# RWKV-7 recurrence with a SoLU MLP on one core: weight fetches moved to another queue and earlier, and four issue orders changed

## The chip, the cores and the metric

The kernel runs on one core of a Trainium2 chip. A core has five engines that each work through their own instruction list in order: TensorE (PE in the profile, with its weight loads as PEld), VectorE (DVE), ScalarE (ACT), GpSimd (POOL) and SyncE (SP), which here only starts transfers. SyncE and ScalarE each have a queue from which they issue DMA transfers (SPq and ACTq in the profile). An engine that meets an instruction whose inputs aren't ready waits, and everything behind that instruction on the same engine waits too. The metric is the device time of one execution in microseconds (us), as the median of several runs.

## The reference

The first block is a linear recurrence over 768 time steps, for 4 batches of 8 heads with head dimension 40. The second is an MLP over the 3072 tokens that come out (320 features each), with 1024 hidden units.

```python
for t in range(S):                       # r, k, v, w, a, b: (4, 8, 768, 40)
    y[:, :, t] = np.einsum('bhd,bhde->bhe', rt, state)
    Sa = np.einsum('bhde,bhe->bhd', state, at)
    state = state * wt[:, :, None, :] - np.einsum('bhd,bhe->bhde', Sa, bt) \
            + np.einsum('bhd,bhe->bhde', vt, kt)
x = y.transpose(0, 2, 1, 3).reshape(3072, 320)
h = x @ w_in                             # 320 x 1024
e = np.exp(h - max(h)); solu = h * e / (sum(e) + 1e-9)
ln = (solu - mean(solu)) / sqrt(var(solu) + 1e-6) * g_ln
out = ln @ w_out                         # 1024 x 320
```

The recurrence's inputs are float32. The two weight matrices arrive as 64-bit floats, and the kernel takes them apart into float32 itself.

## The kernel before

**The recurrence in chunks.** The 768 steps are cut into 12 rounds of 64 steps. A round is done as two *iterations*, each for two of the four batches, so the main loop has N = 24 iterations, i = 0 to 23. Within a chunk the recurrence becomes matrix products and the inverse of triangular 32x32 blocks. For one iteration there are these generator functions, each of which issues a bit of work per step and then yields:

- `front` (letters f and g in the order strings): decay factors, scaled keys, and the triangular blocks `nt`. It runs 5 iterations ahead.
- `scatter` and `gather`: the blocks go through memory so that 64 of them lie one per partition, and come back as `nb`.
- `invert` (I): for a whole round, 30 rows of two VectorE instructions each (L410, L412) on the tile `u`. The result goes to memory in two layouts, and `bring_inverse` fetches it as `tinvT` and `tinv`. Lines 400 to 404 prepare `u`: VectorE fills its first half, GpSimd zeroes its second half (L402) and sets that half's diagonal to one.
- `attend` (a): transposes `kT`, `vT`, `rT` (ScalarE copies them out of PSUM at L259) and the products `psi`, `lamv`, `px0`.
- `solve` (s): completes the 64x64 inverse from 32x32 blocks (`py`, `pz`).
- `recurrence` (r): the serial chain from iteration to iteration. Its first step adds the carried part on VectorE (L525, the tile `x0`, shown as `x`), its third step multiplies by the inverse (`pu`, L544), and later steps update the state `sm`.
- `readout` (y): the outputs of the chunk, multiplied on VectorE (L597, tile `x`) and repacked by DMA for the MLP.

**The MLP.** It runs 6 iterations behind (LAG = 6). `hidden` (h, and b once the iteration is over) has nine steps: five that issue the six products of `h` (L618), the fifth of which also takes the row maximum on VectorE (L628); then the exponential on ScalarE (L632); then q = h times exp on VectorE (L635), written over `e`; then two for the statistics (L640 to L650). The PSUM tile `h` is there only once, so the next MLP's products wait for q. `output` (o) transposes q (L658, copied by ScalarE at L659), multiplies by `w_out` (L663), and scales on ScalarE into `osb` (L668).

**The weights.** `weights` (W) fetches 26 pieces, each into one of four landing tiles, and turns each into float32 by two VectorE instructions (L162, L164), three ScalarE ones (L167 to L169), one more on VectorE (L171) and two on GpSimd (L174, L175). A piece's fetch is issued two pieces ahead, on SyncE's queue (L211). One piece takes two steps of W. After the last, `w_out` is scaled by g and its weighted column mean is taken off: a copy of g (L235), 16 products (`mean`, L238) and eight VectorE instructions (L240).

**The order.** Nothing is scheduled by the compiler: under `manual_schedule` the program order on each engine is what the order strings say. `turns` goes through a string and runs one step of the named generator for each letter (for I the number that `inverse_steps` gives). Iterations 0 to 5 use an EARLY string, later ones STEADY. After the loop six MLPs are left, with a string of their own. Before the loop a prologue computes the first two rounds' fronts, the first inverse and iteration 0's `attend` and `solve`. It is written out in the body of the `with` block:

```python
turns("a a I", dict(I=99), a=at, I=inv)
bring_inverse(0, nc.scalar)
turns("a a a f g f g a f g", {}, f=f, g=g, a=at)
...
ws, after, before = weights(), None, None
```

Here the first inverse is fetched on ScalarE's queue, and `weights` begins only in the loop.

Of the kernel before, what the change touches and what calls it, by code (L numbers as in the profile page):

```python
# [52 lines left out]
def kernel(  # L53
# [94 lines left out]
    def bank(name):  # L148
        return ps1.tile([P, 512], FP32, tag="bank", name=name)
# [28 lines left out]
    def weights():  # L178

        nc.sync.dma_start(out=g_rows, in_=moe_g_ln.rearrange("(c p) -> c p", p=P))
        pieces, hw, hm = [], DFF // 2, DM // 2
        for at in range(0, hw, 256):
            cols = slice(at, at + 256)
            for p in range(2):
                for j in range(2):
                    src = slice(j * hw + at, j * hw + at + 256)
                    pieces.append((w_in[:, 2 * p + j, cols], [moe_w_in[p * hm:p * hm + P, src]]))
            pieces.append((w_in[:, 4, cols], [moe_w_in[p * hm + P:p * hm + hm, j * hw + at:j * hw + at + 256]  # L190
                                              for j in range(2) for p in range(2)]))
        for c in range(NF):
            for at in range(0, DM, 160):
                cols = slice(at, at + 160)
                pieces.append((w2[:, c, cols], [moe_w_out[c * P:(c + 1) * P, cols]]))
        exact = moe_w_in.dtype == FP32
        land, temps = [], []
        if not exact:
            for tag in ("e", "lnT"):
                x = two.tile([P, 512], I64, tag=tag, name="bits", bufs=1)  # L200
                land += [x[:, 0:256], x[:, 256:512]]
            temps = [two.tile([P, 2, 256], I32, tag=tag, name="parts", bufs=1) for tag in ("osb", "parts")]

        def fetch(j):
            if j >= len(pieces):
                return
            dst, parts = pieces[j]
            to = dst if exact else land[j % 4][0:dst.shape[0], 0:dst.shape[1]]
            row = 0
            for part in parts:  # L210
                nc.sync.dma_start(out=to[row:row + part.shape[0]], in_=part)  # L211
                row += part.shape[0]

        for j in range(2):
            fetch(j)
        yield
        open_ = None
        for j, (dst, _) in enumerate(pieces):
            new = None if exact else narrow(dst, land[j % 4], temps[j % 2])
            for _ in range(2):  # L220
                for part in (open_, new):
                    if part:
                        next(part)
                if _:
                    fetch(j + 2)
                yield
            open_ = new
        for _ in range(2):
            if open_:
                next(open_)  # L230
        pg = bank("pg")
        nc.tensor.transpose(out=pg[:, 0:NF], in_=g_rows, identity=ident[0:NF, 0:NF])
        nc.scalar.copy(out=g_col, in_=pg[:, 0:NF])
        gb = two.tile([P, NF, P], FP32, tag="e", name="gb", bufs=1)
        nc.scalar.mul(out=gb, in_=g_col.unsqueeze(2).to_broadcast([P, NF, P]), mul=1.0 / DFF)  # L235
        mean = bank("mean")
        for c in range(NF):
            nc.tensor.matmul(mean[:, 0:DM], lhsT=gb[:, c, :], rhs=w2[:, c, :], start=c == 0, stop=c == NF - 1)  # L238
        for c in range(NF):
            nc.vector.scalar_tensor_tensor(out=w2[:, c, :], in0=w2[:, c, :], scalar=g_col[:, c:c + 1],  # L240
                                           in1=mean[:, 0:DM], op0=ALU.mult, op1=ALU.subtract)
            yield

    def half(p):
        return slice(64 * p, 64 * p + 64)
# [148 lines left out]
    def invert(n):  # L394

        nb = of_round[n]["nb"]
        u = two.tile([P, Q // 2, Q], FP32, tag="u", name="u", bufs=1)
        nc.vector.tensor_scalar(out=u[half(0)], in0=nb[half(0)].rearrange("b (c z) t -> b c z t", z=2)[:, :, 0],  # L400
                                scalar1=-1.0, scalar2=None, op0=ALU.mult)
        nc.gpsimd.memset(u[half(1)], 0.0)  # L402
        for p, engine in enumerate((nc.vector, nc.gpsimd)):
            engine.memset(u[half(p)].rearrange("b c t -> b (c t)")[:, p:Q * Q // 2:Q + 2], 1.0)  # L404
        yield
        for j in range(1, Q - 1):
            m, rows = Q - 1 - j, (j + 1) // 2
            t = two.tile([P, Q * Q // 8], FP32, tag="prod", name="prod", bufs=1)[:, 0:rows * m] \
                .rearrange("p (c r) -> p c r", c=rows)
            nc.vector.tensor_tensor(out=t, in0=nb[:, j:j + 1, j + 1:Q].to_broadcast([P, rows, m]),  # L410
                                    in1=u[:, 0:rows, j:j + 1].to_broadcast([P, rows, m]), op=ALU.mult)
            nc.vector.tensor_tensor(out=u[:, 0:rows, j + 1:Q], in0=u[:, 0:rows, j + 1:Q], in1=t, op=ALU.subtract)  # L412
            yield
        u_dram = of_round[n]["u"] = dram.tile([64, Q, Q], FP32, tag="u_dram", name="u_dram")
        for p in range(2):
            nc.sync.dma_start(out=u_dram.rearrange("b (c z) t -> b c z t", z=2)[:, :, p], in_=u[half(p)])
        ut = two.tile([P, Q, Q // 2], FP32, tag="ut", name="ut", bufs=1)
        nc.vector.tensor_copy(out=ut, in_=u.rearrange("p c t -> p t c"))
        ut_dram = of_round[n]["ut"] = dram.tile([P, Q, Q // 2], FP32, tag="ut_dram", name="ut_dram")
        nc.sync.dma_start(out=ut_dram, in_=ut)  # L420
        yield
# [267 lines left out]
    def fronts(i):  # L689

        return [j for j in ((4, 5) if i == 0 else (i + AHEAD,)) if j < N]

    EARLY = ("r r a r f r W I r W y W r I W W a f L a s W a f W a W I f I W s f W a f",
             "r r a r f g r W I r W y W r I W W a f g L a s W a f g W a W I f g I W s f g W a f g")
    STEADY = "r r b b a r f o r o I o r o y o r I o a f L h a s a h f a I h f I s h f h a f h h"
    front_of = {}

    front_of = {}
# [22 lines left out]
    with tc.manual_schedule():  # L721
        load(0, "w", "a", "b", "k")
        f, g = front(0), front(1)
        turns("f g", {}, f=f, g=g)
        load(1, "w", "a")
        turns("f g", {}, f=f, g=g)
        load(1, "b")
        turns("f f f f g g g g f g", {}, f=f, g=g)
        scatter(0)
        gather(0)  # L730
        load(0, "v", "r")
        load(1, "k")
        f, g, at, inv, so = front(2), front(3), attend(0), invert(0), solve(0)
        turns("f g f g f f g g", {}, f=f, g=g)
        load(2, "w", "a", "b", "k")
        turns("a a I", dict(I=99), a=at, I=inv)
        bring_inverse(0, nc.scalar)
        turns("a a a f g f g a f g", {}, f=f, g=g, a=at)
        scatter(1)
        gather(1)  # L740
        load(1, "v", "r")
        begin(0)
        turns("s s", {}, s=so)
        inv = inverses()
        ws, after, before = weights(), None, None
        for i in range(N):
            m, more, js = i - LAG, i + 1 < N, fronts(i)
            if i % 2 and (i + 3) // 2 < NCH:
                gather((i + 3) // 2)
            if i == 1:  # L750
                steps(inv, 8)
            now = hidden(m) if m >= 0 else None
            parts = dict(r=recurrence(i), y=readout(i), I=inv, W=ws, h=now, b=after, o=before)
            parts.update(zip("fg", (front_of[j] for j in js)))
            if more:
                bring_inverse(i + 1)
                parts.update(a=attend(i + 1), s=solve(i + 1))
            if i % 2 == 0:
                load((i + 6) // 2, "w", "a")
                parts["L"] = later((i + 6) // 2)  # L760
            turns(EARLY[len(js) - 1] if i < LAG else STEADY, dict(I=inverse_steps(i)), **parts)
            if i % 2:
                load((i + 3) // 2, "v", "r")
                repack(i // 2)
            if js and js[-1] % 2:
                scatter(js[-1] // 2)
            begin(i + 1)
            after, before = now, output(m) if m >= 0 else None
            if i == LAG - 1:
                steps(ws, 99)  # L770
        for m in range(N - LAG, N):
            now = hidden(m)
            turns("h h o o h h b b h o o o o h h", {}, h=now, b=after, o=before)
            after, before = now, output(m)
        turns("b b o o o o o o", {}, b=after, o=before)


# [28 lines left out]
```

## Time and profile before

The median is 848.69 us of 3 runs (846.84 to 854.91). The profiled execution spans 844.7 us. The trace was cut into stages at the first `pu` product of each iteration:

| stage | us | PE busy | DVE busy | granted PE clock |
|---|---|---|---|---|
| prologue, to the `pu` of iteration 0 | 0 to 66.7 | 25.2 | 26.8 | 0.74 |
| iteration 0 | 66.7 to 116.5 | 21.4 | 22.9 | 0.66 |
| iteration 1 | 116.5 to 151.3 | 18.7 | 20.0 | 0.75 |
| iterations 2 to 4 | 151.3 to 238.5 | 58.2 | 57.0 | 0.66 to 0.73 |
| iterations 5 and 6 | 238.5 to 297.9 | 43.3 | 34.0 | 0.82 and 0.99 |
| two steady iterations | 572.6 to 627.3 | 50.0 | 35.0 | 0.97 |
| iterations 19 to 22 | 627.3 to 723.4 | 85.0 | 46.7 | 0.97 |
| the last six MLPs | 738.7 to 844.7 | 78.5 | 29.9 | 0.85 |

Read it thus: where PE is busy for most of a stage (steady: 50.0 of 54.7 us), only PE's own gaps can be won. Where it isn't (everything up to iteration 5, and the end), the stage is as long as a chain through several engines and transfers, and the question is which wait ends last. The granted clock is the share of full speed that TensorE was given in the stage.

### The profile page before, as it was taken

To read this page: it belongs to the slowest core of one execution; us is meant where nothing else is said; L and a number is where in the kernel's file an instruction comes from. 1 tells how busy PE (TensorE), PEld (TensorE's weight loads), DVE (VectorE), ACT (ScalarE), POOL (GpSimd) and SP (SyncE) were. 2 spreads that over 40 slices of the span, in tenths; PEclk is the share of its full clock that TensorE was granted. 3 is DMA by queue.
4 is the path that set the end of the run, shared out by engine and by line. 5 is a ranking of instruction groups with operands and counts; after the bars stand their busy time and mean duration, and the time that the engine had idled before them with its cause. 6 is when DMAs were issued, how large, how long until landed. Compare 5 with 4: busy or idle time off the path is not lost.

```text
span 844.7 us, 28254 instructions
## 1 busy us (share of the span) xinstructions
PE 646.6 (77%) x12281; PEld 462.1 (55%) x12281; DVE 451.1 (53%) x1234; ACT 272.3 (32%) x631; POOL 126.3 (15%) x228
## 2 busy tenths in 40 slices
PE   6124364685666998989989989899898998868786
PEld 4123353564455666666666666566665666534343
DVE  3352484756744756666577575674766633332222
ACT  4012333343432333433443334433343323211211
POOL 4101323331330120111201110111001000000000
PEclk9658567776778998999999999999999999979878
DMA  9815535444561453534534435435134111000000
GB/s 133 134 35 101 117 64 109 93 94 102 104 116 26 78 100 53 109 70 84 104 64 87 88 61 102 84 72 101 21 79 73 43 34 25 15 21 1 16 16 16
DMA packets 269804, 60.02 MB, mean 71 GB/s; under 512 B 255464, under 2 KB 265328, under 8 KB 269680
## 3 DMA queue, kind: packets, MB, share of 16 engines
q1 hardware_dynamic: 268448, 57.91, 36.6%
q8 instruction: 97, 1.59, 0.8%
q10 hardware_dynamic: 1232, 0.30, 0.2%
q14 instruction: 27, 0.22, 0.1%
HBM read 40.08 MB, written 13.37 MB: 63 GB/s over the span
## 4 chain that ended last, share of the span: by engine, by line
PE 59%; DVE 14%; SPq 8%; DMA 6%; issue 6%; ACT 5%; POOL 0%; ACTq 0%; DVEq 0%; POOLq 0%
PE h L618 13%; PE po L663 13%; PE plnT L658 4%; DVE u L412 3%; DVE prod L410 3%; PE pcx L337 3%; DVE e L635 3%; PE pyo L590 2%; SPq L302 2%; PE py L478 2%; PE pst L570 2%; PE pu L544 2%; PE plamv L276 2%; PE pyo L504 2%; DVE nmax L628 2%
## 5 line engine op out<-in xcount | busy, mean ns | idle before, releaser
L618 PE MATMUL h<-w_in,xT 128*128 128x512 f32 (+1 forms) x288 | 135.5, 673 | 19.6 <-DVE e L635 16.5
L663 PE MATMUL po<-w,lnT 128*128 128x320 f32 x384 | 120.4, 446 | 0.0
L410 DVE TENSOR_TENSOR prod<-blk,u 128x30 f32<-128x30 f32 (+4 forms) x360 | 98.8, 274 | 29.5 <-POOL u L404 17.5
L412 DVE TENSOR_TENSOR u<-u,prod 128x30 f32<-128x30 f32 (+4 forms) x360 | 102.2, 284 | 12.4
L663 PEld LDWEIGHTS po<-w,lnT 128*128 128x128 f32 x384 | 69.2, 194 | 24.3 <-issue 3.5
L650 POOL TENSOR_TENSOR rs<-c,mhalf 128x1 f32<-128x1 f32 x24 | 13.2, 549 | 371.1 <-DVE c L649 348.4
L618 PEld LDWEIGHTS h<-w_in,xT 128*128 128x128 f32 (+1 forms) x288 | 40.1, 201 | 45.8 <-issue 42.3
L337 PE MATMUL pcx<-cst,lw 128*128 128x132 f32 x192 | 35.7, 320 | 27.1 <-ACT vT L259 22.8
L668 ACT ACTIVATE osb<-po,rs 128x320 f32<-128x320 f32 x24 | 12.6, 527 | 134.2 <-PE po L663 122.1
L628 DVE TENSOR_REDUCE nmax<-h 128x1 f32<-128x1024 f32 x24 | 29.3, 1223 | 48.9 <-PE h L618 48.9
L635 DVE TENSOR_TENSOR e<-h,e 128x1024 f32<-128x1024 f32 x24 | 29.4, 1225 | 44.1 <-ACT e L632 44.1
L337 PEld LDWEIGHTS pcx<-cst,lw 128*128 128x128 f32 x192 | 29.9, 215 | 39.3 <-ACT vT L259 23.2
L544 PE MATMUL pu<-tinvT,x 64*64 64x64 f32 x768 | 21.0, 250 | 36.4 <-DVE x L525 25.5
L659 ACT COPY lnT<-plnT 128x512 f32<-128x512 f32 x48 | 27.8, 587 | 63.2 <-PE plnT L658 62.9
L278 DVE TENSOR_TENSOR lamv<-plamv,cst 128x512 f32<-128x512 f32 x24 | 16.6, 692 | 56.5 <-PE plamv L276 56.5
L278 DVE TENSOR_TENSOR lamu<-plamu,cst 128x512 f32<-128x512 f32 x24 | 16.6, 691 | 48.2 <-PE plamu L276 48.2
L478 PE MATMUL py<-tinv,nt 32*32 32x32 f32 x768 | 19.8, 204 | 29.2 <-ACT vT L259 19.2
L544 PEld LDWEIGHTS pu<-tinvT,x 64*64 64x64 f32 x768 | 17.4, 155 | 42.5 <-DVE x L525 29.7
L658 PE MATMUL plnT<-cst,e 128*128 128x128 f32 x192 | 38.1, 342 | 3.2 <-DVE e L635 3.2
L597 DVE TENSOR_TENSOR x<-pyo,kx 128x512 f32<-128x512 f32 x24 | 16.6, 690 | 43.2 <-PE pyo L590 42.9
L276 PE MATMUL plamv<-rT,vT 64*64 64x64 f32 x768 | 19.1, 246 | 26.7 <-ACT rT L259 26.4
L658 PEld LDWEIGHTS plnT<-cst,e 128*128 128x128 f32 x192 | 29.0, 177 | 14.7 <-issue 10.7
(108 smaller groups left out, 1163.5 us busy)
## 6 DMA issues: line engine op xcount, KB each, us to landing
blk<-blk_dram SPq DMA_DIRECT2D x24, 256.0 KB
raw_w<-in_w_dram SPq DMA_DIRECT2D x24, 160.0 KB
raw_a<-in_a_dram SPq DMA_DIRECT2D x24, 160.0 KB
raw_b<-in_b_dram SPq DMA_DIRECT2D x24, 160.0 KB
raw_k<-in_k_dram SPq DMA_DIRECT2D x24, 160.0 KB
v<-in_v_dram SPq DMA_DIRECT2D x24, 160.0 KB
r<-in_r_dram SPq DMA_DIRECT2D x24, 160.0 KB
out_dram<-osb SPq DMA_DIRECT2D x24, 160.0 KB
```

The lines of the kernel that those rows point to most:

```text
L276: nc.tensor.matmul(t[half(c ^ p * cross), p, g * L:(g + 1) * L], lhsT=lhs[half(p), g, half(c)], rhs=rhs[half(p), g, half(c)], start=True, ...
L278: nc.vector.tensor_tensor(out=dst, in0=t[:, :, 0:G * L].rearrange("q p (g c) -> q p g c", g=G), in1=tri.unsqueeze(1).unsqueeze(1).to_broad ...
L337: nc.tensor.matmul(t[:, g * 132:g * 132 + 132], lhsT=pair(lw, 2 * j + g), rhs=cst[:, lo:lo + 132], start=True, stop=True)
L410: nc.vector.tensor_tensor(out=t, in0=nb[:, j:j + 1, j + 1:Q].to_broadcast([P, rows, m]), in1=u[:, 0:rows, j:j + 1].to_broadcast([P, rows, ...
L412: nc.vector.tensor_tensor(out=u[:, 0:rows, j + 1:Q], in0=u[:, 0:rows, j + 1:Q], in1=t, op=ALU.subtract)
L478: nc.tensor.matmul(t[quarter(out), c:c + Q], lhsT=lhs(p, g), rhs=rhs(p, g), start=True, stop=True)
L544: nc.tensor.matmul(t[half(z), c ^ p, h // 2 * L:h // 2 * L + L], lhsT=x0[half(c ^ p), h, :], rhs=d["tinvT"][half(c ^ p), p, h % G, :], sta ...
L618: nc.tensor.matmul(h[:, j * 512:j * 512 + 512], lhsT=of_round[i // 2]["xT"][rows, kt, i % 2 * P:i % 2 * P + P], rhs=w_in[rows, 4 if kt == ...
L628: nc.vector.tensor_reduce(out=nmax, in_=h, axis=AX.X, op=ALU.max, negate=True)
L635: nc.vector.tensor_tensor(out=q, in0=h, in1=e, op=ALU.mult)
L658: nc.tensor.transpose(out=t[:, j * P:(j + 1) * P], in_=q[:, f * P:(f + 1) * P], identity=ident)
L663: nc.tensor.matmul(o[:, 0:DM], lhsT=lnT[:, f, :], rhs=w2[:, f, :], start=f == 0, stop=f == NF - 1)
```

## The change

It has five parts, all of them of order or of the engine used; the arithmetic stays as it was.

1. The weights' transfers (32 fetches and g) are issued by ScalarE instead of SyncE. The first W step, which fetches g and the first two pieces, moves from iteration 0 into the prologue, so that the first piece has landed when it is needed. The EARLY strings have nine W each instead of ten.
2. In the prologue, `psi` and `rT` are issued before the first inverse is fetched on ScalarE's queue instead of after it; the other steps of `attend` alternate with the fronts.
3. In `invert`, the second half of `u` is cleared, and given its diagonal, on VectorE instead of GpSimd (for all twelve inverses).
4. In STEADY, q (the seventh step of `hidden`) moves behind the recurrence's first step of the next iteration, so that VectorE does the `x0` addition before q. The first step of `hidden` moves ahead. The steps `b` follow later. The centring of `w_out` gets two more yields (ahead of the mean's products and after them) and then takes two pieces per step; what is left of it when iteration 6 begins is issued there.
5. In the last six MLPs, the exponential is issued ahead of the four last `output` steps, and with that ahead of `osb`, instead of after them; q follows at the start of the next one.

```diff
-        nc.sync.dma_start(out=g_rows, in_=moe_g_ln.rearrange("(c p) -> c p", p=P))
+        nc.scalar.dma_start(out=g_rows, in_=moe_g_ln.rearrange("(c p) -> c p", p=P))
...
-                nc.sync.dma_start(out=to[row:row + part.shape[0]], in_=part)
+                nc.scalar.dma_start(out=to[row:row + part.shape[0]], in_=part)
...
         nc.scalar.mul(out=gb, in_=g_col.unsqueeze(2).to_broadcast([P, NF, P]), mul=1.0 / DFF)
+        yield
         mean = bank("mean")
         for c in range(NF):
             nc.tensor.matmul(mean[:, 0:DM], lhsT=gb[:, c, :], rhs=w2[:, c, :], start=c == 0, stop=c == NF - 1)
+        yield
         for c in range(NF):
             nc.vector.scalar_tensor_tensor(out=w2[:, c, :], in0=w2[:, c, :], scalar=g_col[:, c:c + 1],
                                            in1=mean[:, 0:DM], op0=ALU.mult, op1=ALU.subtract)
-            yield
+            if c % 2:
+                yield
...
-        nc.gpsimd.memset(u[half(1)], 0.0)
-        for p, engine in enumerate((nc.vector, nc.gpsimd)):
-            engine.memset(u[half(p)].rearrange("b c t -> b (c t)")[:, p:Q * Q // 2:Q + 2], 1.0)
+        nc.vector.memset(u[half(1)], 0.0)
+        for p in range(2):
+            nc.vector.memset(u[half(p)].rearrange("b c t -> b (c t)")[:, p:Q * Q // 2:Q + 2], 1.0)
...
-    EARLY = ("r r a r f r W I r W y W r I W W a f L a s W a f W a W I f I W s f W a f",
-             "r r a r f g r W I r W y W r I W W a f g L a s W a f g W a W I f g I W s f g W a f g")
-    STEADY = "r r b b a r f o r o I o r o y o r I o a f L h a s a h f a I h f I s h f h a f h h"
+    EARLY = ("r r a r f r W I r y W r I W W a f a s W a f W a W I f I W s f L W a f",
+             "r r a r f g r W I r y W r I W W a f g a s W a f g W a W I f g I W s f g L W a f g")
+    STEADY = "r b r a r f b b o r o I o r o y o r I o h a f L a s a h f a I h f I s h f h a f h"
...
-        f, g, at, inv, so = front(2), front(3), attend(0), invert(0), solve(0)
+        f, g, at, inv, so, ws = front(2), front(3), attend(0), invert(0), solve(0), weights()
...
-        turns("a a I", dict(I=99), a=at, I=inv)
+        turns("a a I a a W", dict(I=99), a=at, I=inv, W=ws)
         bring_inverse(0, nc.scalar)
-        turns("a a a f g f g a f g", {}, f=f, g=g, a=at)
+        turns("a f g a f g f g", {}, f=f, g=g, a=at)
...
+            if i >= LAG:
+                steps(ws, 99)
...
-            if i == LAG - 1:
-                steps(ws, 99)
...
-            turns("h h o o h h b b h o o o o h h", {}, h=now, b=after, o=before)
+            turns("b h h o o h h b b h h o o o o", {}, h=now, b=after, o=before)
...
-        turns("b b o o o o o o", {}, b=after, o=before)
+        turns("b b b o o o o o o", {}, b=after, o=before)
```

More of the change, by code (lines that the diff above doesn't have):

```diff
@@ L691, in fronts @@
         return [j for j in ((4, 5) if i == 0 else (i + AHEAD,)) if j < N]
-    EARLY = ("r r a r f r W I r W y W r I W W a f L a s W a f W a W I f I W s f W a f",
-             "r r a r f g r W I r W y W r I W W a f g L a s W a f g W a W I f g I W s f g W a f g")
-    STEADY = "r r b b a r f o r o I o r o y o r I o a f L h a s a h f a I h f I s h f h a f h h"
+    EARLY = ("r r a r f r W I r y W r I W W a f a s W a f W a W I f I W s f L W a f",
+             "r r a r f g r W I r y W r I W W a f g a s W a f g W a W I f g I W s f g L W a f g")
+    STEADY = "r b r a r f b b o r o I o r o y o r I o h a f L a s a h f a I h f I s h f h a f h"
+    front_of = {}
     front_of = {}
@@ L744 @@
         inv = inverses()
-        ws, after, before = weights(), None, None
+        after, before = None, None
         for i in range(N):
```

## The prediction

> **What bounds the kernel now.** I read the slices first, then the waits, then the timeline at three places, and last the busy time and clock by stretches.
>
> ```profile
> PE   6124364685666998989989989899898998868786
> ...
> PEclk9658567776778998999999999999999999979878
> ```
>
> Each digit is a fortieth of the span, 21 us. PE is 90% busy from about 290 to 690 us only. Before that and in the last 105 us it is idle a third to two thirds of the time, at a reduced clock. So the first 276 us and the end hang on chains, and the middle on PE and its few gaps. The table of waits names what ends them (total, times, longest):
>
> ```profile
> ACT rT L259 <- DMA tinv<-ut_dram: 27.2, 1, 27.2
> ...
> DVE parts L162 <- DMA bits<-in_moe_w_in_dram: 18.2, 2, 11.3
> ...
> PE pu L544 <- DVE x L525: 25.5, 13, 2.7
> ```
>
> The first lies in the prologue, the second in iterations 0 and 1, the third once in each of iterations 7 to 19. In iterations 20 to 23 the same gap ahead of `pu` is booked as "issue", 10.8 us in 4. The prologue's timeline (start, duration, idle time before in brackets):
>
> ```profile
> 33.14 0.52 POOL L402 MEMSET u<- 64x512 f32 x1
> ...
> 33.87 0.19 DVE L410 TENSOR_TENSOR prod<-blk,u 128x30 f32<-128x30 f32 x1 [8.87 <-POOL u L404]
> ...
> 56.76 0.58 ACT L259 COPY rT<-prT 128x512 f32<-128x512 f32 x1 [27.21 <-DMA tinv<-ut_dram]
> ```
>
> VectorE is ready for the inverse's rows at 25.0 but waits 8.87 us: GpSimd clears `u` only after two key products that wait for `raw_k`. Then ScalarE stands at the fetch of the inverse, and with it `rT` and all behind it. In the steady stage:
>
> ```profile
> 598.20 1.22 DVE L635 TENSOR_TENSOR e<-h,e 128x1024 f32<-128x1024 f32 x1 [0.67 <-ACT e L632]
> ...
> 599.34 0.48 DVE L525 TENSOR_TENSOR x<-x_own,px 128x320 f32<-128x320 f32 x1
> ...
> 599.87 0.61 PEld L544 LDWEIGHTS pu<-tinvT,x 64*64 64x64 f32 x32 [2.91 <-DVE x L525]
> ```
>
> The `x0` addition stands behind q, which waits for the exponential, while PE waits. And in the last MLPs:
>
> ```profile
> 755.05 0.53 ACT L668 ACTIVATE osb<-po,rs 128x320 f32<-128x320 f32 x1 [6.36 <-PE po L663]
> 755.47 1.11 ACT L632 ACTIVATE e<-h,nmax 128x1024 f32<-128x1024 f32 x1
> ...
> 758.07 3.74 PE L618 MATMUL h<-w_in,xT 64*128 64x512 f32 x6 [3.12 <-DVE e L635]
> ```
>
> The exponential's input is ready at 751.9, but it stands behind `osb`, which waits for PE's last product; then PE waits 3.12 us for q.
>
> **What the Trainium skill says.** "TensorE: Matmul & The Clock Gate", section "What's actually happening": TensorE falls to half clock after an idle window of about 3.4 us and is back after as long a busy one. The trace agrees in the main: the granted clock is 0.50 from 742.5 to 746.4, after a gap of 3.90 us, 0.58 from 758 to 762 after 3.12, 0.50 from 786 to 790; but 1.00 from 772.7 to 778 after 3.19. "DMA: Bandwidth & Descriptors", section "Issuing engines are not separate DMA queues": issuing from a second engine saves only the issuing time, the transfers share the same DMA engines. So part 1 must be paid for by queueing alone. The trace shows that: SyncE issues the first two pieces at 84.57, behind a dozen other transfers, and VectorE has waited since 76.8. "Perfetto Trace Analysis", section "DMA Instruction — HWDGE (DVE, Sync)": the issuing sequencer is held until all descriptors are made. Here that is 0.42 us (median) for a w_in fetch, 0.37 for a w_out one, and 0.46 for the four `tinv` fetches on ScalarE's own queue.
>
> **The change part by part.**
>
> *Prologue.* The clear on VectorE costs 0.49 us (VectorE's own 128x512 memset, 485 ns; GpSimd's 0.52 bounds it above) and the second diagonal 0.07. So rows start at 25.6 instead of 33.87: 8.3 us. They take 17.0 us as before, to 42.6; their result was in memory 3.95 us after the last row (50.86 to 54.8), so at 46.5; the four fetches take 1.83 us to issue, to 48.4. The second gain is order: `rT` is now copied near 31, and `lamv`, `paT` need no ScalarE after that. Behind the fetch remain `x_own` 0.42, two `bT` copies 1.09 and the products `pnt` 0.7. So `py` comes at about 50.8 instead of 63.87: 13 us. Taken alone, the clear gives 8.3; I take 13. The three weight issues (1.3 us) fall at 31 to 33, where ScalarE has 15 us to spare: nothing.
>
> *Weights, iteration 0.* VectorE's wait of 11.25 us before 88.07 goes, since the piece is fetched 25 us before its use. Behind that wait stood rows of the inverse, and ScalarE with `vT` at 95.12, for which PE waited 22 us: it is on the path. Less one issue ahead of `vT`: 10.7.
>
> *Iteration 1.* The second such wait, 6.96 us before 136.42, arose because the fetch stood behind the next inverse's on SyncE. It goes too, but `py` (138.41) needs `tinv`, whose issue ended at 132.67, some 2 us before landing: 4.
>
> *Issues on ScalarE.* 30 fetches at about 0.4 us in iterations 0 to 5 make 12 us. ScalarE is 40% busy there (11.8 of 29 us), but about a third stand straight ahead of an `a` copy that PE awaits: +4. A fetch also waits for its landing tile; SyncE's waits of that kind were 5.4 us at most, and the pieces' readers come two W steps earlier, so I take nothing; this is the slower rival. Nine W instead of ten per iteration only shifts work.
>
> *Centring.* PE waited 6.7 us for `gb` before `mean` (7.1 us, stays). The new yield lets PE do other work, but ScalarE still waits for VectorE's L171 at `gb`, and eight instructions of 0.54 us now stand ahead of `x0` in iteration 6, 1.5 us past what PE has to do: -2 net, between -6 and +3.
>
> *Steady.* With q behind it, `x0` needs `px` and VectorE free. In iteration 17 it could run from 570.25, and PE is then bound by its own products to 571.23 instead of 572.59: 1.34. In iteration 18 the maximum and `nt` keep VectorE to 597.5, `x0` ends at 598.0, PE starts at 598.05 instead of 599.87: 1.82. q starts when it did, because the exponential ends it (570.88, 598.16), and its next readers, the transposes, come at 572.8 and 599.7, after q's ends at 572.1 and 599.4. Mean 1.58, times 13 iterations: 20.5. The clear on VectorE, 0.56 us per 55, is hidden: VectorE is idle 20 us of 54.7.
>
> *Iterations 20 to 23.* PE has less to do there, and after `pu` the transposes wait for q. In iteration 21 they start at 676.45 instead of 677.57, in the others, whose gaps were 3.9, near 2 us earlier: 6 in all.
>
> *Last MLPs.* The chain maximum 1.22, exponential 1.3, q 1.23 with its hand-overs takes 3.86 us (738.66 to 742.52), started 0.2 after `po`; `po` lasts 4.47. So it lies beside `po`, by 0.4 us. Five gaps of 3.12 to 3.19 and the last of 3.19 go: 18.8. The first (3.90) stays, with no `po` behind it. Then the clock: after gaps the first six h records took 4.08, 3.74, 2.18, 4.08, 3.93, 4.08, where 2.18 is at full clock; without the first, 7.1 to win, and about 2 from transposes (1.04 at full clock, up to 1.92 here): 9.
>
> Sum: -13 -10.7 -4 +4 -2 -20.5 -6 -18.8 -9 = -80. From the median, 848.7 - 80 = 769.
>
> SyncE's later `L` is free: without the weights nothing stands between the two places in its queue.
>
> **Rivals.**
> - *The early gains are given back.* Transfers or ScalarE's longer list set the pace of iterations 0 to 5, so that of the 25.7 net up to iteration 6 little is left. For it: DMA is over 80% busy in the first 42 us, and PE waits for `vT` copies 5 to 8 us in iterations 2 to 4 too. Against: both big waits are single, with one cause. Without that part: 848.7 - 54 = 794.
> - *The steady gap turns into another.* The transposes wait for q, or VectorE's rows come between; against it, 0.3 to 0.7 us of slack in both iterations looked at. With a quarter of the 20.5: 784. With both rivals: 810.
> - *Slower.* ScalarE stands at each fetch for its landing tile. With the longest seen, 5.4 us, 24 times: +130, so 769 + 130 = 899. For it: GpSimd waits long for ScalarE's `inv` and frees the tiles late. Against: SyncE's waits of this kind (for L171 and the GpSimd steps on `parts`) sum to 15 us in 8 cases.
>
> **How the numbers follow.** The main case 0.64, early gains lost 0.16, steady gap replaced 0.12, both 0.04, slower 0.04. Within the main case the open terms are the prologue (8.3 to 13.2), the issues (0 to 12), the centring (-6 to +3) and the clock (0 to 11; more if the early stage's 0.66 to 0.75 rises too): about 750 to 787. The range reaches to the first two rivals: 748 to 800. Faster by over 1%: 0.94; within 1%: 0.02; slower: 0.04.
>
> **What would show it.** The first row at 25.6, and `pu` of iteration 0 near 54. No wait of L162 for `bits` above 1 us. ScalarE's waits ahead of L211: sum under 10 us; if over 50, the slower rival. `pu` after `x` under 1 us per iteration and a pitch near 25.7 instead of 27.4. `h` never waiting for q in the last MLPs but for the first, at a pitch of about 10 us and a clock near 1. Wrong it would be most of all if PE's time freed at one place is waited away at the next.

## The result, and the profile after

The median fell from 850.28 us (4 runs, 846.84 to 854.91) to 758.39 us (4 runs, 757.23 to 763.0): ratio 0.8926, with a 95% interval of 0.8867 to 0.8985. The forecast was 769 us, in a range of 748 to 800. The profiled executions span 844.7 and 757.1 us. Cut at the first `pu` of each iteration as before, their difference of 87.6 us lies here (the rounded stages sum to 87.5):

| stage | before, us | after, us | difference | forecast |
|---|---|---|---|---|
| prologue | 66.7 | 57.9 | -8.8 | -13 |
| iteration 0 | 49.8 | 37.5 | -12.3 | -10.7 |
| iteration 1 | 34.7 | 32.0 | -2.7 | -4 |
| iterations 2 to 4 | 87.2 | 91.0 | +3.8 | +4, for 0 to 5 |
| iterations 5 and 6 | 59.4 | 61.1 | +1.7 | -2 |
| iterations 7 to 19 | 354.4 | 319.6 | -34.8 | -20.5 |
| iterations 20 to 22 | 71.1 | 67.0 | -4.1 | -6, with 23 |
| `pu` of 23 to the end | 121.3 | 91.0 | -30.3 | -27.8 |

A stage of one trace is known to about 1 us: iterations 2 to 4 took 85.4 to 87.2 us in the traces of four kernels that are alike up to there, and `pu` of iteration 0 came between 57.9 and 59.1 in six with the changed prologue (in two of them the weights are fetched on SyncE's queue).

The slices of the page, each now 19 us long:

```profile
PE   6335758566584899999999999999999899998997
...
PEclk9656575795775799999999999999999999999999
```

PE now stays at 80% or more from about 246 us to the slice before the last, from about 265 us on at a clock of 0.9 or more. Ahead of that it is as holed as before; between the `pu` of iterations 0 and 6 the granted clock is even a little lower (0.69, before 0.72). The table of waits (total, times, longest):

```profile
ACT x L465 <- DMA tinv<-ut_dram: 19.3, 1, 19.3
...
PE py L481 <- DMA tinv<-ut_dram: 17.8, 3, 8.1
...
PEld pu L547 <- DVE x L528: 10.9, 10, 2.5
```

Each line gives who waited, at which line of the kernel, and for what. The line in which VectorE waited for the weights' `bits` (18.2 us) is gone. The fetch of the first inverse still stops ScalarE, but `rT` is no longer what stands behind it. `pu` behind the `x0` addition fell from 29.7 us (the page's figure for the weight loads) to 10.9. New is the middle line: `py` waits for a later inverse in iterations 1, 3 and 5, up to 8.1 us. No step of the forecast has it.

The prologue's timeline (start, duration, idle time before in brackets):

```profile
25.14 0.48 DVE L405 MEMSET u<- 64x512 f32 x1 [0.16 <-issue]
...
31.18 0.58 ACT L262 COPY rT<-prT 128x512 f32<-128x512 f32 x1 [1.47 <-PE prT L260]
...
31.64 0.28 DVE L415 TENSOR_TENSOR u<-u,prod 128x120 f32<-128x120 f32 x1
31.75 1.75 POOL L330 TENSOR_TENSOR kx<-raw_k,inv 128x320 f32<-128x320 f32 x2 [12.20 <-DMA raw_k<-in_k_dram]
...
31.95 0.82 DVE L413 TENSOR_TENSOR prod<-blk,u 128x114 f32<-128x114 f32 x1
...
48.33 2.65 ACTq L434 DMA_DIRECT2D tinv<-ut_dram  x4
...
51.99 1.99 PE L279 MATMUL pnt<-kx,bT 64*64 64x64 f32 x64 [3.12 <-ACT bT L262]
...
53.91 1.06 PE L481 MATMUL py<-tinv,nt 32*32 32x32 f32 x32
```

The clear no longer waits for GpSimd, and rows start at 25.94. `rT` is copied at 31.18 instead of 56.76. But GpSimd's key products now run beside the rows: a row's instruction takes 0.82 us next to one, against 0.28 just before. And the four fetches take 2.65 us to issue, where 1.83 were forecast.

The steady stage, from the same view:

```profile
551.10 0.48 DVE L528 TENSOR_TENSOR x<-x_own,px 128x320 f32<-128x320 f32 x1
...
551.63 0.75 PE L547 MATMUL pu<-tinvT,x 64*64 64x64 f32 x32 [0.76 <-DVE x L528]
...
551.86 1.22 DVE L638 TENSOR_TENSOR e<-h,e 128x1024 f32<-128x1024 f32 x1 [0.28 <-ACT e L635]
```

Now the addition comes first and q after it, and q still waits for nothing but the exponential. Before, the gaps of PE ahead of `pu` were 1.36 and 2.67 us in turn; now they are none and 0.76. Two steady iterations and the last six MLPs by stretches (length, busy time of PE, PEld, DVE, ACT and POOL, granted clock, DMA share, GB/s):

```profile
526.70:576.10 49.40, 48.19 (x1045) 34.27 (x1044) 35.72 (x98) 20.11 (x47) 6.75 (x11) 1.00 0.33 65
...
681.20:757.10 75.90, 66.47 (x240) 38.60 (x240) 29.95 (x56) 19.72 (x35) 3.83 (x7) 0.96 0.08 20
```

The pair takes 49.4 us instead of 54.7. PE's idle time in it fell by 3.5 us (4.7 to 1.2), and its *busy* time by 1.8 (50.0 to 48.2) for the same products: they ran faster. The last MLPs come every 9.9 us instead of every 13 to 16, at a clock of 0.96 instead of 0.85.

### The profile page after: what moved, and what is told of

Same layout as the page of the kernel before. It is cut to its first block, busy times and chain, and to the rows that moved or that the text cites. A ratio compares the mean times of both kernels' runs of the same rounds, so it can differ in the third digit from the quotient of the medians.

```text
span 757.1 us, 28253 instructions
## 1 busy us (share of the span) xinstructions
PE 630.4 (83%) x12281; PEld 451.1 (60%) x12281; DVE 455.5 (60%) x1258; ACT 270.1 (36%) x631; POOL 118.4 (16%) x204
## 4 chain that ended last, share of the span: by engine, by line
PE 65%; DVE 17%; DMA 6%; ACT 5%; issue 4%; SPq 2%; ACTq 0%; POOL 0%; DVEq 0%
PE po L666 14%; PE h L621 14%; DVE prod L413 5%; DVE u L415 5%; PE plnT L661 3%; PE pyo L593 3%; PE pcx L340 3%; PE plamv L279 2%; PE pst L573 2%; PE pcum L327 2%; DMA blk<-blk_dram 2%; PE py L481 2%; DMA blk_dram<-nt 2%; PE pyo L507 2%; PE px L526 1%
## 5 line engine op out<-in xcount | busy, mean ns | idle before, releaser
L621 PE MATMUL h<-w_in,xT 128*128 128x512 f32 (+1 forms) x288 | 126.8, 627 | 3.9 <-DVE e L638 3.9
L666 PE MATMUL po<-w,lnT 128*128 128x320 f32 x384 | 118.8, 442 | 0.0
L415 DVE TENSOR_TENSOR u<-u,prod 128x30 f32<-128x30 f32 (+4 forms) x360 | 98.3, 273 | 12.4
L330 POOL TENSOR_TENSOR kx<-raw_b,inv 128x320 f32<-128x320 f32 x24 | 20.9, 873 | 255.2 <-ACT inv L328 204.6
L621 PEld LDWEIGHTS h<-w_in,xT 128*128 128x128 f32 (+1 forms) x288 | 37.8, 189 | 30.6 <-issue 28.7
L481 PE MATMUL py<-tinv,nt 32*32 32x32 f32 x768 | 21.1, 207 | 29.7 <-DMA tinv<-ut_dram 17.8
L635 ACT ACTIVATE e<-h,nmax 128x1024 f32<-128x1024 f32 x24 | 26.7, 1114 | 37.3 <-DVE nmax L631 37.3
L653 POOL TENSOR_TENSOR rs<-c,mhalf 128x1 f32<-128x1 f32 x24 | 13.2, 548 | 157.0 <-DVE c L652 157.0
L481 PEld LDWEIGHTS py<-tinv,nt 32*32 32x32 f32 x768 | 17.8, 118 | 32.0 <-issue 18.5
L496 ACT ACTIVATE tinvT<-pz 32x256 f32<-32x256 f32 x48 | 17.9, 373 | 51.3 <-PE pz L481 51.0
L661 PE MATMUL plnT<-cst,e 128*128 128x128 f32 x192 | 30.6, 290 | 5.7 <-DVE e L638 5.4
L580 POOL TENSOR_TENSOR sm<-tot,fac 128x320 f32<-128x320 f32 x20 | 14.7, 737 | 118.6 <-DVE tot L579 98.7
```

The source lines that it names most:

```text
L481: nc.tensor.matmul(t[quarter(out), c:c + Q], lhsT=lhs(p, g), rhs=rhs(p, g), start=True, stop=True)
L621: nc.tensor.matmul(h[:, j * 512:j * 512 + 512], lhsT=of_round[i // 2]["xT"][rows, kt, i % 2 * P:i % 2 * P + P], rhs=w_in[rows, 4 if kt == ...
L635: nc.scalar.activation(out=e, in_=h, func=AF.Exp, bias=nmax, accum_out=esum)
L661: nc.tensor.transpose(out=t[:, j * P:(j + 1) * P], in_=q[:, f * P:(f + 1) * P], identity=ident)
L666: nc.tensor.matmul(o[:, 0:DM], lhsT=lnT[:, f, :], rhs=w2[:, f, :], start=f == 0, stop=f == NF - 1)
```

## The experiments

The theory after this result: each part removes its own wait, the parts add, and closing a gap of PE also gives back the half clock that followed it. The main rivals: the parts depend on each other; the queue rather than the early start is what helps; the early stage stayed long because PE's clock is low there, or because something new delays the inverse. Times below are medians; ratios are to the kernel before, measured beside each.

**One part alone, on the kernel before.** First the last MLPs (run e1_tail):

```diff
-            turns("h h o o h h b b h o o o o h h", {}, h=now, b=after, o=before)
+            turns(("b " if m > N - LAG else "") + "h h o o h h b b h h o o o o", {}, h=now, b=after, o=before)
...
-        turns("b b o o o o o o", {}, b=after, o=before)
+        turns("b b b o o o o o o", {}, b=after, o=before)
```

> The kernel before with part 5 alone (the exponential ahead of the last output steps in the last six MLPs). My sum: 18.8 us of waits plus 9 us of half clock, so about 28 us less than before, near 822, and a pitch of 9.9 us in the last MLPs with a granted clock of 0.95 or more there. Rival, that the clock has no part in it and the rest came from elsewhere: 19 us less, near 831, at a pitch near 12.

Measured: 817.69 us, ratio 0.9626 (0.9598 to 0.9653), a gain of 31.7. The last six MLPs take 76.0 us at a clock of 0.94, and the stage from `pu` of 23 to the end 91.4 instead of 121.3. Part 5 stands by itself.

The steady order alone (e2_steady: STEADY of the change, and the `b` that the first of the last MLPs then needs):

```diff
-    STEADY = "r r b b a r f o r o I o r o y o r I o a f L h a s a h f a I h f I s h f h a f h h"
+    STEADY = "r b r a r f b b o r o I o r o y o r I o h a f L a s a h f a I h f I s h f h a f h"
```

> The kernel before with the new STEADY string alone (and q as first step of the first of the last MLPs). By my record, 1.6 us per iteration: 27 us less in all with iterations 20 to 23. By the theory formed after the result, that the gap ahead of pu also cost half clock behind it, two iterations take 49.4 instead of 54.7 us and the whole gain is 35 to 40 us, near 812. Rival, that the steady gain needs the other parts (less traffic on SyncE's queue): 20 us or less.

Measured: 808.12 us, 0.9513 (0.9473 to 0.9553), a gain of 41.3. The pair takes 49.4 us, as in the changed kernel, and iterations 7 to 19 take 319.6 us, as there: the whole -34.8 comes from this order.

The clear alone (e3_clear):

```diff
-        nc.gpsimd.memset(u[half(1)], 0.0)
+        nc.vector.memset(u[half(1)], 0.0)
...
-            engine.memset(u[half(p)].rearrange("b c t -> b (c t)")[:, p:Q * Q // 2:Q + 2], 1.0)
+            nc.vector.memset(u[half(p)].rearrange("b c t -> b (c t)")[:, p:Q * Q // 2:Q + 2], 1.0)
```

> The kernel before with part 3 alone (u cleared on VectorE). The inverse's first row starts near 25.9 instead of 33.87; rT, still behind the fetch on ScalarE, moves with it, so 6 to 8 us less, near 842. Rival, that the wait for the first weight piece in iteration 0 takes the gain back, since its fetch is paced by SyncE's queue and not by the inverse: 0 to 2 us less.

Measured: 839.56 us, 0.989 (0.9863 to 0.9917). `pu` of iteration 0 starts at 60.0 instead of 66.7: 6.7 us, not 8.3. The rows run from 26.06 to 44.29, 18.2 us instead of 17.0, with two instructions of 0.97 and 0.82 us among them.

What is left, parts 1 and 2 with the centring and the EARLY strings, without the clear, STEADY and the tail (e5_early):

```diff
-                nc.sync.dma_start(out=to[row:row + part.shape[0]], in_=part)
+                nc.scalar.dma_start(out=to[row:row + part.shape[0]], in_=part)
...
-    EARLY = ("r r a r f r W I r W y W r I W W a f L a s W a f W a W I f I W s f W a f",
+    EARLY = ("r r a r f r W I r y W r I W W a f a s W a f W a W I f I W s f L W a f",
...
-        turns("a a I", dict(I=99), a=at, I=inv)
+        turns("a a I a a W", dict(I=99), a=at, I=inv, W=ws)
```

> The kernel before with parts 1 and 2 and the new centring and EARLY strings, without the clear on VectorE, the new STEADY and the new order of the last MLPs. If the parts add up, it is what the three parts measured alone leave of the whole: 91.5 less 31.7, 41.3 and 9.8, about 9 us less than before, near 841. My record gave 17 us net to these parts beyond the clear; if that holds here, near 832.

Measured: 838.06 us, 0.988 (0.9848 to 0.9913), a gain of 10.0. Sum of the four: 31.7 + 41.3 + 9.8 + 10.0 = 92.8, against 91.9 between the two medians; by the profiled spans 29.6 + 42.2 + 6.9 + 8.8 = 87.5, against 87.6. The parts add, within what these runs can tell; none needs another.

**The half clock behind the gap.** Here `pu` of the kernel before still waits for `x0`, but in the steady iterations three more products are issued ahead of it, whose result nobody reads (e4_fill):

```diff
+        for _ in range(3 if i > LAG else 0):
+            nc.tensor.matmul(t[:, 0, 256:512], lhsT=ident, rhs=cst[:, 0:256], start=True, stop=True)
```

> The kernel before with three products of 128x128 by 128x256 that nobody reads, put on PE right ahead of pu in iterations 7 to 23 (into unused columns of pu's tile). They fill the gap without shortening the wait. If the gap costs half clock behind it, the clock in the steady stage rises from 0.97 to near 1.00 and two iterations take 53 to 54 instead of 54.7 us: 5 to 12 us less in all. If the clock has no part in it, the time stays or rises by up to 10 us.

Measured: 836.15 us, 0.9839 (0.9808 to 0.9871): 13.2 us faster by adding work. In the traces, iterations 7 to 19 take 344.1 us instead of 354.4. PE's timeline behind a short gap and behind the long gap that comes next, in the kernel before:

```profile
572.59 0.75 PE L544 MATMUL pu<-tinvT,x 64*64 64x64 f32 x32 [1.36 <-DVE x L525]
...
599.87 0.75 PE L544 MATMUL pu<-tinvT,x 64*64 64x64 f32 x32 [2.67 <-DVE x L525]
600.55 1.12 PE L324 MATMUL pcum<-lw,cst 128*128 128x320 f32 x2
601.46 1.06 PE L658 MATMUL plnT<-cst,e 128*128 128x128 f32 x4
```

and with the gap filled:

```profile
590.30 1.56 PE L540 MATMUL pu<-cst 128*128 128x256 f32 x6 [0.38 <-DVE nt L278]
...
592.60 0.75 PE L546 MATMUL pu<-tinvT,x 64*64 64x64 f32 x32 [0.73 <-DVE x L525]
593.27 0.81 PE L324 MATMUL pcum<-lw,cst 128*128 128x320 f32 x2
593.92 0.60 PE L660 MATMUL plnT<-cst,e 128*128 128x128 f32 x4
```

Two iterations of the filled kernel as a stretch:

```profile
563.80:616.90 53.10, 51.26 (x1058) 36.55 (x1057) 34.97 (x96) 20.43 (x47) 7.38 (x13) 1.00 0.30 61
```

`pu` waits for the same addition, but the two groups behind it take 0.81 and 0.60 us instead of 1.12 and 1.06, and the clock of the pair is 1.00 instead of 0.97. So the pair takes 53.1 instead of 54.7. This is the main part of the steady gain that the forecast lacked. Only the longer gap has this after-effect: in iterations 7 to 18 of the kernel before, the first group of transposes (`plnT`) took 0.90 to 1.06 us behind each of the six gaps of 2.67, and 0.60 behind each of the six of 1.36. The granted clock was 0.56 from 600.5 to 603.9 us, and 1.00 from 573.2 to 576.0, behind the short gap. With the gap filled, it was 1.00 from 593.2 to 596.2.

**The early stage: queue, clock, centring, loads.** These four start from the changed kernel. First, the weights go back to SyncE's queue, but start as early as now (e6_sync):

```diff
-                nc.scalar.dma_start(out=to[row:row + part.shape[0]], in_=part)
+                nc.sync.dma_start(out=to[row:row + part.shape[0]], in_=part)
```

> The changed kernel with the weights' transfers back on SyncE's queue, everything else as changed. If ScalarE's queue is what removes the waits, the wait for the first piece in iteration 0 or the one in iteration 1 comes back and the time rises by 5 to 15 us. If the early start alone does it (the rival, and what my record charges ScalarE with, 4 us of issues), the time stays within 4 us or falls a little.

Measured: 760.99 us, 0.8962 (0.892 to 0.9003). The intervals overlap with the changed kernel's; 2.6 us between the medians. Iteration 0 has no wait for the weights' `bits` here either: that wait went because the first piece is fetched in the prologue. In iteration 1 a wait of 5.4 us comes back (7.0 in the kernel before), so the queue does remove it, but iteration 1 takes 31.6 us with it and 32.0 without: it is not on the path. From the `pu` of iteration 0 to that of iteration 6 it takes 199.3 us, and 199.7 in the changed kernel.

The old centring, without the two yields, one piece per step (e7_centre):

```diff
-            if c % 2:
-                yield
+            yield
...
-            if i >= LAG:
-                steps(ws, 99)
...
+            if i == LAG - 1:
+                steps(ws, 99)
```

> The changed kernel with the centring as before: no yield ahead of the mean's products or after them, one piece per step, the rest at the end of iteration 5. My record gave the new centring 2 us of gain; by the trace iterations 5 and 6 took 61.2 us after, 59.4 before. If the new centring is what costs, 2 to 4 us less; if it gains, 2 us more.

Measured: 758.05 us, 0.8926 (0.8887 to 0.8966): no difference.

Ten unread products in each of iterations 0 to 5, spread over `attend`, `solve` and `recurrence`, so that the clock stays up (nobody reads them; e8_warm):

```diff
+    def warm(t, n=2):
+        for _ in range(n if early[0] else 0):
+            nc.tensor.matmul(t[:, 0, 256:512], lhsT=ident, rhs=cst[:, 0:256], start=True, stop=True)
...
+        if name in ("psi", "lamv"):
+            warm(t)
```

> The changed kernel with two products of 128x128 by 128x256 that nobody reads ahead of psi, lamv, px0, px and pu in iterations 0 to 5, ten per iteration. If half clock lengthens the early chain, the granted clock there rises from 0.64 to 0.73 towards 0.9 and the stage from the pu of iteration 0 to that of iteration 6 (199.7 us) gets 5 to 15 us shorter. If these iterations hang on transfers and on VectorE, the time stays or rises by up to 15 us (ten times 0.5 us in each of six iterations is 30 us of PE work, most of it in gaps).

Measured: 766.6 us, 0.9042 (0.8983 to 0.91). The clock between the `pu` of iterations 0 and 6 rose from 0.69 to 0.82, and that stage grew from 199.7 to 203.6 us. `pu` of iteration 0, behind two of the products, came at 59.73 instead of 57.88. So a higher clock by this means doesn't shorten the stage, and what filled a gap in the steady stage stands in the way here. What the low clock costs by itself is not shown, since the added products stand on the path too.

Last, the letter L (the loads of a later front) back where it was in the two EARLY strings, ahead of the inverse's last steps (e9_load):

```diff
-    EARLY = ("r r a r f r W I r y W r I W W a f a s W a f W a W I f I W s f L W a f",
+    EARLY = ("r r a r f r W I r y W r I W W a f L a s W a f W a W I f I W s f W a f",
```

> The changed kernel with L (the loads of b and k) back at its earlier place in the two EARLY strings. My record called the move free. By the trace the loads now stand on SyncE's queue behind the inverse's write and ahead of the blocks' scatter, gather and the fetch of tinv, for which py waits 17.8 us in three iterations. If that is the cause, those waits go, and the time falls by 8 to 15 us. Rival, that the waits for tinv come from the inverse's rows being late: no change.

Measured: 747.44 us, 0.8814 (0.8763 to 0.8866), 11 us less than the changed kernel. The stage takes 189.0 us instead of 199.7: iteration 3 26.2 instead of 32.1, iteration 5 35.7 instead of 39.3. (Three more traces with the late loads, e6_sync, e7_centre and e12_pool, have 198.9 to 199.6; e10_last, with the early ones, 189.8.) SyncE's queue in the changed kernel:

```profile
157.02 0.62 SPq L423 DMA_DIRECT2D ut_dram<-ut  x1
157.75 1.41 SPq L305 DMA_DIRECT2D raw_b<-in_b_dram  x2
159.25 1.78 SPq L305 DMA_DIRECT2D raw_k<-in_k_dram  x2
161.12 4.69 SPq L388 DMA_DIRECT2D blk_dram<-nt  x4
169.31 1.12 SPq L395 DMA_DIRECT2D blk<-blk_dram  x2
170.54 2.01 SPq L434 DMA_DIRECT2D tinv<-ut_dram  x4
```

and at the same place with L early:

```profile
143.95 1.31 SPq L305 DMA_DIRECT2D raw_k<-in_k_dram  x2
...
156.13 0.63 SPq L423 DMA_DIRECT2D ut_dram<-ut  x1
156.86 2.12 SPq L388 DMA_DIRECT2D blk_dram<-nt  x4
161.00 1.91 SPq L395 DMA_DIRECT2D blk<-blk_dram  x2
162.95 2.06 SPq L434 DMA_DIRECT2D tinv<-ut_dram  x4
```

From the start of the inverse's write to the first issue that fetches it (L423 to L434) the changed kernel needs 13.5 us, this one 6.8. In the first, four loads stand ahead of the scatter (L388). Its issue then takes 4.69 us instead of 2.12, the gather (L395) waits for it, and the fetch of the inverse stands behind the gather. `py`, which waited 8.1 us for that fetch, waits 0.8 and 1.3 here in this iteration; in iteration 5 it waits 3.1 instead of 4.9. The wait of iteration 1 stays (4.4 instead of 4.8), so it has another cause.

With L early, the queue was tried once more, with the weights on SyncE, the edit of e6_sync on top of e9_load (e11_load_sync):

> The changed kernel with the loads back at their earlier place and the weights' transfers on SyncE's queue. With the late loads the queue made no difference that could be measured. If SyncE's queue stands in the way once the loads are early (the weights' waits hold up tinv and the blocks), 3 to 10 us more than 747.4; if only the early start counts, within 3 us of it.

Measured: 751.01 us, 0.886 (0.8829 to 0.8892), 3.6 more than with ScalarE's queue. Against e9_load the intervals still overlap; in the trace the early stage is 192.9 us against 189.0 and 189.8 (e9_load, e10_last). So ScalarE's queue may be worth some 3 us once the loads are early; one trace doesn't settle it.

**VectorE beside GpSimd.** The two key products that GpSimd makes in the prologue are each made three times (the same values, so nothing else changes); one run, e12_pool:

```diff
-        grown(0, "k")
+        for _ in range(3 if i in (2, 3) else 1):
+            grown(0, "k")
```

> The changed kernel with the two key products of the prologue that run on GpSimd beside the first inverse done three times each (same result). In the changed kernel the two rows beside them took 0.82 us an instruction instead of 0.28, and the rows 18.5 us in all instead of 17.0. If VectorE and GpSimd hold each other up, eight instructions or so take 0.8 us, the rows take 20 to 21 us and the pu of iteration 0 comes about 2 us later; if the two long instructions had another cause, the rows stay at 18.5 us.

Measured: 761.11 us in one run; in its trace the rows take 20.9 us instead of 18.4 (18.3 to 18.6 in the six other traces with this prologue and the clear on VectorE). `pu` of iteration 0 comes at 60.2: 2.3 us later than in the changed kernel, 1.0 later than the latest of five others.

```profile
31.36 5.48 POOL L330 TENSOR_TENSOR kx<-raw_k,inv 128x320 f32<-128x320 f32 x6 [12.48 <-DMA raw_k<-in_k_dram]
...
35.15 0.89 DVE L414 TENSOR_TENSOR prod<-blk,u 128x119 f32<-128x119 f32 x1
36.08 0.90 DVE L416 TENSOR_TENSOR u<-u,prod 128x119 f32<-128x119 f32 x1
37.01 0.29 DVE L414 TENSOR_TENSOR prod<-blk,u 128x128 f32<-128x128 f32 x1
```

Six instructions of the rows fall beside the six products, and each takes 0.83 to 0.96 us; the first after them takes 0.29. The Trainium skill, "SBUF — State Buffer", section "Who interferes with whom", says that a VectorE instruction with two inputs in SBUF contends with a GpSimd instruction that reads SBUF, and that the ports which the two share are an exclusive lock. The trace agrees on VectorE's side: GpSimd's products take 0.91 us each here, and a row's instruction about as long as one of them. GpSimd itself lost little: its two products took 1.67 us in the kernel before, where VectorE stood idle, and 1.75 in the changed one.

**One step further.** On top of e9_load, the last iteration of the loop, in which no front is left, gets a string of its own (e10_last): `hidden` comes earlier, and the last two `output` steps stand behind its products:

```diff
+    LAST = "r b r r b b o r o o r o y r h h h h h o h o"
...
-            turns(EARLY[len(js) - 1] if i < LAG else STEADY, dict(I=inverse_steps(i)), **parts)
+            turns(EARLY[len(js) - 1] if i < LAG else STEADY if more else LAST, dict(I=inverse_steps(i)), **parts)
```

> The changed kernel with the loads of b and k back at their earlier place (747.4 us alone) and, in iteration 23 only, two steps of the last output moved behind the products of h, so that PE has 2.4 us of work in the one gap of 3.9 us that is left ahead of the last MLPs. 2 to 4 us less, near 744, if the gap closes and no half clock follows it; no change if the exponential then comes later by as much.

Measured: 744.91 us, 0.8791 (0.8752 to 0.8829), the fastest kernel here, 13.5 us below the changed one. PE behind the first gap of the last MLPs, with e9_load:

```profile
673.43 2.87 PE L621 MATMUL h<-w_in,xT 64*128 64x512 f32 x6 [3.90 <-DVE e L638]
676.09 1.91 PE L661 MATMUL plnT<-cst,e 128*128 128x128 f32 x8
```

and with the string:

```profile
669.09 2.32 PE L666 MATMUL po<-w,lnT 128*128 128x320 f32 x8
...
673.15 2.19 PE L621 MATMUL h<-w_in,xT 64*128 64x512 f32 x6 [1.75 <-DVE e L638]
```

The gap is 1.75 us instead of 3.90, and the records behind it are back at full speed (2.19 us instead of 2.87). From `pu` of 23 to the end it takes 87.0 us instead of 91.1. The 2.5 us between the medians are within the runs' scatter; the trace shows the gain, the times alone don't.

## Why the prediction was right, and where its steps were off

**Last MLPs: right.** Forecast -27.8, measured -30.3, and -29.9 in the trace of part 5 alone. The pitch is 9.9 us as said, and the first gap stayed at 3.90 as said. In the last six MLPs PE's idle time fell by 18.0 us (18.8 were reckoned) and its busy time by 12.1 (the clock's term was 9).

**Steady: right mechanism, too small a size.** "-20.5" counted only idle time between PE's instructions. The idle term was fair: 3.5 us per pair where 2 x 1.58 were forecast. Missing is the low clock behind the longer gap of each pair, 1.8 us of PE's busy time per pair. The last MLPs were given a clock term of 9; the steady gaps got none, though the same records (1.12 and 1.06 us for groups of 0.81 and 0.60) stood in the trace of before. The prediction gives no reason for leaving it out. The idle window that it cites from the Trainium skill ("TensorE: Matmul & The Clock Gate", "What's actually happening") is about 3.4 us, longer than these gaps. Here a gap of 2.67 us was enough, one of 1.36 was not, and e4_fill shows that the gap is the cause. Length alone doesn't decide it: the gap of 3.19 us ahead of 772.7 was followed by full clock.

**Iterations 20 to 23.** -6 was forecast for the four, -4.1 measured for the first three. The working takes their gaps as 3.9 us but for one; in the trace they are 3.90, 2.16, 2.16 and 2.60.

**Prologue: terms that were too small, and a low clock.** "Rows start at 25.6" was right within 0.4. "17.0 us as before" was wrong by 1.4, since the earlier start puts the rows beside GpSimd's products (e12_pool shows the effect). "The four fetches take 1.83 us to issue" was wrong by 0.8 in this trace. Why is open: e7_centre and e9_load, with the same prologue, took 1.87 and 1.85. That SyncE issues fetches of `tinvT` at the same time is not enough to explain it, for it did so before too (from 54.21, ScalarE from 54.88). So `py` comes at 53.91 instead of 50.8. Behind it a third thing: PE had waited 3.12 us ahead of `pnt`, and `pnt`, `py` and what follows ran at a granted clock of 0.50 (1.99 and 1.06 us, where they took 1.43 and 0.74 with the clear alone); from `py` to `pu` it is 4.0 us instead of 2.8. Of the -8.8, the clear alone gives 6.7 (e3_clear) and the order without it 1.2 (e5_early).

**Weights: right in size, the queue beside the point.** -12.3 and -2.7 where -10.7 and -4 were forecast; e6_sync leaves the early start as the cause. For iteration 1 the working took 132.67 as the end of the issues of `tinv`; that is `tinvT`, and those of `tinv` ended at 130.70. ScalarE did not stand at a fetch: its waits ahead of L211 last 38 ns at most, so the slower rival is out. Its 5.4 us was misread as well: that was a wait of a load (L302); SyncE's waits ahead of a weight fetch (L211) were 1.9 us at most.

**The +4: right number, wrong reason.** It was put down to issues that stand ahead of ScalarE's copies. Iterations 2 to 4 did lose 3.8 us, but e9_load takes that back and more (84.5 us for the three, against 87.2 before and 91.0) with every issue of the weights still on ScalarE. The step that failed is the last one: "SyncE's later `L` is free: without the weights nothing stands between the two places in its queue." The inverse's two writes stand between them, and they wait for VectorE. Once behind them, the loads start later (`raw_k` at 159.25 instead of 143.95 in the iteration shown) and stand ahead of the scatter, the gather and the next fetch. It cost about 11 us, of which nothing was forecast. It was hidden in the total since the steady stage gave 14 more than was reckoned. Up to the `pu` of iteration 7, 18.3 us were won of the 25.7 reckoned. That the total comes near the forecast, 87.6 against 80, is in part luck: two errors of opposite sign.

**Centring.** -2 was forecast, nothing was measured (e7_centre). Iterations 5 and 6 lost 1.7 us; with the loads early they take 56.5 instead of 61.1.

**The rivals.** "Early gains given back" was partly true: all of parts 1 and 2 with the centring and the strings brings 10.0 us. What iterations 2 to 6 gave back was due neither to the weights' transfers nor to ScalarE's list, but to one letter. The rival of a new steady gap and the slower one were wrong. What stays open: why the early stage, even with L early, takes 26 to 37 us per iteration, where a steady one takes 24.7. A higher clock by added products didn't shorten it (e8_warm, with L late), nor did the other queue for the weights (e11_load_sync).

## What to carry to other kernels

On a queue that issues in order, moving an issue behind one that waits changes the start of everything behind it; before calling such a move free, list what stands between the two places and what each of them waits for. Where an engine has two operations to do, put first the one that is ready and that the bounding engine waits for, if the other's readers come later. When a gap of PE is closed, price the slow products behind it too: compare the same group just behind a gap and far from one.

## What the runs showed of the hardware that was not expected

- In a stream that is otherwise busy, a gap of 2.67 us was followed by slow groups each time in iterations 7 to 18 (0.90 to 1.06 us instead of 0.60, granted clock 0.56 over the 3.4 us looked at), a gap of 1.36 us never. Three unread products in the gap made the whole kernel 13.2 us faster; ten per iteration where PE waits for other engines made it about 8 slower.
- An instruction of VectorE with two inputs took 0.82 to 0.97 us instead of 0.28 beside a GpSimd product of 0.86 to 0.91 us.
